# Sparse attention and experts on one core: local queries in a block-diagonal tile of their own, filled by GpSimd, and their transfers on ACT's queue

## Chip, cores and metric

One core of a Trainium2 chip. The metric is the device time of one execution in microseconds (us); lower is better. Times are medians of runs of the same program.

## What is computed

Eight batches, eight heads, 576 positions, head size 64. Heads 0 to 3 see a local window of 32 keys, heads 4 to 7 every 32nd key. The result of attention is read as 4608 tokens of 512 values, each of which goes to one of eight experts (512 to 1024, ReLU, back to 512), scaled by its gate. All is in fp32.

```python
scores = scale * np.matmul(q, k.transpose(0, 1, 3, 2))
mask_local = (rel >= 0) & (rel < stride)                      # stride 32, heads 0 to 3
mask_strided = (rel >= 0) & (pos[None, :] % stride == pos[:, None] % stride)
attn = softmax(np.where(masks, scores, -1e9)); x = attn @ v   # x as (4608, 512)
e = argmax(x @ w_gate); gate = softmax(x @ w_gate)[e]
out = gate * (np.maximum(x @ w1[e], 0.0) @ w2[e])
```

## The kernel before

**Tasks.** Attention is 40 tasks: batch b from 0 to 7, and in each five PSUM banks k from 0 to 4 (`BANK_PAIRS`, L54). Task n is 5 x b + k. Banks 0 and 1 hold the local scores of two heads each (heads 0 and 1, heads 2 and 3), banks 2 to 4 the last local blocks and the strided scores. Each task goes through three stages:

- `stage_s` (L388): TensorE adds the mask into the bank by a matmul (L391), then the scores. For local banks this is `wide` (L396): per block j of 32 queries one matmul, whose weights are 128 rows x 64 columns: the queries of head 0 in the upper 64 rows of 32 columns, of head 1 in the lower 64 rows of the other 32, zeros elsewhere (block diagonal). Each of these fp32 matmuls shows as two passes, so a task has 32. Then `softmax` (L337): VectorE's maximum and subtract, ACT's exponent, VectorE's sum and reciprocal, GpSimd's multiply of 128x512 (L350).
- `stage_t` (L438): four transposes of the probabilities (L441), copied out of PSUM by ACT (L443, L444, L447).
- `av_local` (L457, matmuls at L466) and `av_strided` (L470): probabilities times values, into xT.

**Where the local queries lie before.** For each of the two local banks there is one fixed tile `qkl[k]` (L355): 512 columns for head 0's queries, 512 for head 1's, then 544 of keys. The halves that must be zero are cleared once (L358 on VectorE, L359 on GpSimd). A load is three transfers on SP's queue (L369 to L371): the lower 64 rows of the second queries and keys in one, the upper 64 rows of the first queries, the upper 64 rows of the keys. The host has laid the queries out so that block j is every 16th column; `wide` reads its weights with that step:

```python
q = qkl[k][:, 0:2 * LQ].rearrange("p (q j) -> p q j", j=LB)      # LB = 16
nc.tensor.matmul(sb[64 * i:64 * i + 64, col:col + 64], q[:, :, j], qkl[k][:, k0:k0 + 64], ...)
```

**What sets the order.** TensorE's order is that of the loop at L803, written by hand: in turn i, `stage_t` of task i - 3, steps of routing, `stage_s` of task i, the values of task i - 4, a filling of expert work from the fifth batch on. The loads of queries and keys for task i + 5 are called right behind `stage_s` of task i (L821), those of values at L831. The other engines' queues, ACT, VectorE, GpSimd and SP, are put in order by a scheduler that goes by its own estimates of time; each engine then works its queue strictly in turn. `raw` tiles of expert weights (1 MB each, L204) are loaded by SP too, and split by `wsplit` (L209) into a rounded part (a cast on ACT, L212) and a rest (a subtract on VectorE, L213). Two raw and two split tiles exist in this part. Behind attention come the windows of the experts (`window`, L255) and eight slots for what is left over (`slot`, L872).

## Time and profile before

| | us |
|---|---|
| median of 3 runs | 691.83 |
| lowest, highest | 690.89, 695.33 |
| the profiled execution | 688.08 |
| its span in the trace | 686.2 |
| attention with its fillings, about | 0 to 215 |
| experts, about | 215 to 686 |

Times in the trace count from the start of its span; 1.9 us of the profiled execution lie outside it. PE is TensorE's matmuls, PEld its weight loads, DVE VectorE, ACT ScalarE, POOL GpSimd, SP SyncE; a q behind a name is that engine's queue of issues. A line number is that of the kernel above. In the trace a wait is put down to the event that ended it.

### The profile page before, as it was taken

How to read it: one execution, taken by the hardware profiler on the slowest of the kernel's cores; microseconds unless marked ns; L12 is line 12 of the kernel's file. 1: busy time of each engine (PE TensorE's matmuls, PEld its weight loads, DVE VectorE, ACT ScalarE, POOL GpSimd, SP SyncE). 2: the span in 40 equal slices, each digit the busy share in tenths (PEclk: the TensorE clock that was granted, in tenths of full speed). 3: DMA queues.
4: the chain of work that ended last, by engine and by line, in shares of the span. 5: the costliest groups of instructions: out<-in, count | busy, mean ns of one | idle time of the engine just before them, and what ended most of it. 6: DMA issues, size and time to landing. Idle time of an engine off the chain costs nothing.

```text
span 686.2 us, 14770 instructions
## 1 busy us (share of the span) xinstructions
PE 648.9 (95%) x5996; PEld 542.4 (79%) x5996; DVE 431.2 (63%) x796; ACT 354.5 (52%) x617; POOL 150.7 (22%) x168
## 2 busy tenths in 40 slices
PE   4999999799889899999999999999999999999997
PEld 3876768587778688897888988878888878988885
DVE  5667878567835579796336775346675248683364
ACT  1556666565555544564337574246473247572362
POOL 3222223511321302053005132022032041100021
PEclk9899999999999999999999999999999999999999
DMA  9879998985645657469327867337675257664140
GB/s 281 244 225 262 331 307 247 349 300 169 217 176 206 240 187 251 159 238 342 140 92 266 296 245 261 118 124 262 261 257 208 107 191 264 258 218 170 66 180 21
DMA packets 36695, 149.85 MB, mean 218 GB/s; under 512 B 5261, under 2 KB 5645, under 8 KB 26384
## 3 DMA queue, kind: packets, MB, share of 16 engines
q1 hardware_dynamic: 24576, 118.50, 51.1%
q0 software_dynamic: 6432, 20.26, 8.1%
q10 hardware_dynamic: 5616, 10.12, 4.1%
q8 instruction: 48, 0.79, 0.5%
q14 instruction: 23, 0.19, 0.1%
HBM read 129.69 MB, written 20.22 MB: 218 GB/s over the span
## 4 chain that ended last, share of the span: by engine, by line
PE 74%; issue 12%; DVE 5%; ACT 4%; DMA 2%; POOL 1%; POOLq 1%; SPq 0%; another core or an unknown queue 0%
PE t L287 8%; PE t L289 8%; PE t L288 8%; PE y L276 6%; PE y L278 6%; PE y L277 6%; PE s L399 4%; PE t L441 2%; PE s L412 2%; PE v L455 2%; PE v L466 2%; PE s L276 2%; PE s L278 2%; PE s L277 2%; PE v L265 2%
## 5 line engine op out<-in xcount | busy, mean ns | idle before, releaser
L213 DVE TENSOR_TENSOR wlo<-raw,whi 128x1024 fp32r<-128x1024 f32 x160 | 192.7, 1222 | 86.9 <-ACT whi L212 75.6
L212 ACT CAST whi<-raw 128x1024 fp32r<-128x1024 f32 x160 | 163.2, 1050 | 67.1 <-PE s L278 26.1
L287 PE MATMUL t<-xh,whi 128*128 128x256 f32 (+1 forms) x384 | 125.2, 327 | 1.9 <-ACT xh L221 1.3
L288 PE MATMUL t<-xl,whi 128*128 128x256 f32 (+1 forms) x384 | 123.8, 323 | 0.3 <-DVE xl L222 0.3
L289 PE MATMUL t<-xh,wlo 128*128 128x256 f32 (+1 forms) x384 | 123.4, 322 | 0.1
L292 ACT ACTIVATE hh<-t 128x256 fp32r<-128x256 f32 (+1 forms) x96 | 43.5, 453 | 115.1 <-PE t L289 109.2
L293 DVE SCALAR_TENSOR_TENSOR hl<-t,hh 128x256 fp32r<-128x256 f32 (+1 forms) x96 | 49.0, 510 | 75.6 <-ACT hh L292 75.2
L287 PEld LDWEIGHTS t<-xh,whi 128*128 128x128 f32 x384 | 72.4, 189 | 9.8 <-ACT xh L221 1.8
L288 PEld LDWEIGHTS t<-xl,whi 128*128 128x128 f32 x384 | 72.6, 189 | 7.2 <-DVE xl L222 0.7
L289 PEld LDWEIGHTS t<-xh,wlo 128*128 128x128 f32 x384 | 72.5, 189 | 6.4 <-DVE wlo L213 0.9
L276 PE MATMUL y<-whi,hh 128*128 128x512 f32 x192 | 76.2, 397 | 0.0
L277 PE MATMUL y<-wlo,hh 128*128 128x512 f32 x192 | 75.0, 391 | 0.0
L278 PE MATMUL y<-whi,hl 128*128 128x512 f32 x192 | 75.0, 396 | 0.0
L248 POOL DMA_INDIRECT out_dram<-y,oids x24 | 26.9, 1121 | 215.1 <-DVE y L247 166.5
L350 POOL TENSOR_TENSOR prob<-prob,ri 128x512 f32<-128x512 f32 x40 | 42.5, 1062 | 121.8 <-DVE ri L349 94.1
L155 ACT COPY xT<-v 128x270 f32<-128x270 f32 (+1 forms) x80 | 30.0, 481 | 29.0 <-PE v L455 13.0
L278 PEld LDWEIGHTS y<-whi,hl 128*128 128x128 f32 x192 | 35.6, 188 | 8.3
L276 PEld LDWEIGHTS y<-whi,hh 128*128 128x128 f32 x192 | 36.0, 188 | 6.7 <-ACT hh L292 0.7
L277 PEld LDWEIGHTS y<-wlo,hh 128*128 128x128 f32 x192 | 36.1, 188 | 5.7
L346 DVE TENSOR_REDUCE sm<-prob 128x8 f32<-128x512 f32 x40 | 27.3, 683 | 20.6 <-ACT prob L344 20.4
L340 DVE TENSOR_REDUCE nm<-s 128x8 f32<-128x512 f32 x40 | 27.3, 683 | 18.8 <-PE s L399 14.2
L344 ACT ACTIVATE prob<-prob 128x512 f32<-128x512 f32 x40 | 25.2, 631 | 22.9 <-DVE prob L343 22.1
(173 smaller groups left out, 1167.2 us busy)
## 6 DMA issues: line engine op xcount, KB each, us to landing
raw<-in_wcat_dram SPq DMA_DIRECT2D x80, 1024.0 KB, 6.5
xd<-xr ACTq DMA_DIRECT2D x36, 264.0 KB, 4.8
vl<-in_vv_dram SPq DMA_DIRECT2D x16, 512.0 KB, 6.5
qkl<-in_qk_dram SPq DMA_DIRECT2D x16, 264.0 KB, 3.8
vt<-in_vv_dram SPq DMA_DIRECT2D x16, 256.0 KB, 4.7
qk<-in_qk_dram SPq DMA_DIRECT2D x8, 484.0 KB, 5.5
qk<-in_qk_dram SPq DMA_DIRECT2D x8, 432.0 KB, 4.9
qk<-in_qk_dram SPq DMA_DIRECT2D x8, 396.0 KB, 6.3
```

What stands on the lines that cost most here:

```text
L155: nc.scalar.copy(out=out, in_=in_)
L212: nc.scalar.copy(out=hi[:, sl], in_=raw[:, sl])
L213: i = nc.vector.tensor_tensor(out=lo[:, sl], in0=raw[:, sl], in1=hi[:, sl].bitcast(F32), op=ALU.subtract)
L276: nc.tensor.matmul(yb[t], hh[:, ts], whi[:, w], start=(j == 0), stop=False)
L277: nc.tensor.matmul(yb[t], hh[:, ts], wlo[:, w], start=False, stop=False)
L278: nc.tensor.matmul(yb[t], hl[:, ts], whi[:, w], start=False, stop=(j == 7))
L287: nc.tensor.matmul(hb[:, 0:n], whi[:, w], xh[:, dc, :], start=(dc == 0), stop=False)
L288: nc.tensor.matmul(hb[:, 0:n], whi[:, w], xl[:, dc, :], start=False, stop=False)
L289: nc.tensor.matmul(hb[:, 0:n], wlo[:, w], xh[:, dc, :], start=False, stop=(dc == 3))
L292: nc.scalar.activation(out=hh[:, 0:n], in_=hb[:, 0:n], func=AF.Relu)
L293: nc.vector.scalar_tensor_tensor(out=hl[:, 0:n], in0=hb[:, 0:n], scalar=0.0, in1=hh[:, 0:n].bitcast(F32), op0=ALU.max, op1=ALU.subtract)
L350: lastp[0] = nc.gpsimd.tensor_tensor(out=pv, in0=pv, in1=ri.unsqueeze(2).broadcast_to([128, 8, 64]), op=ALU.mult)
```

## The change

- The local queries and keys come in one transfer of 128 rows x 1056 columns per task into `qkl[k]`, without gaps for zeros. For batch 0 SP issues it, from batch 1 on ACT.
- A new tile `qbd[k]` per local bank holds the block diagonal, block by block: 16 blocks of 64 columns. It is cleared once by VectorE. A new function `spread` copies each head's 64 rows of queries into their places by GpSimd, two copies of 64x512 per task; it is called for task i + 2 behind `stage_s` of task i, and for tasks 0 and 1 ahead of the loop.
- `wide` reads its weights from one block of `qbd[k]`, 64 columns in one run, and its keys from `qkl[k]`. The host no longer permutes the queries.
- The tiles of the other banks' queries and values become one per bank instead of three in rotation, and one small tile of the slot tables becomes a scratch tile.

```diff
--- before.py
+++ after.py
@@ -41,6 +41,7 @@
 CHW = 2 * 1024
 LAG_T = 3
 LAG_AV = 4
+AHEAD = 2
 EXP = (0, 2, 4, 6)
 EG = NG // 2
 EARLY = (3, 1, 2)
@@ -306,7 +307,7 @@
         return window(e, [ids[:, t, e:e + 1] for t in tr], [oids[:, t, e:e + 1] for t in tr], gpool, xpool, ypool)
 
     with ExitStack() as actx:
-        inp = actx.enter_context(tc.tile_pool(name="inp", bufs=NBK - 2))
+        inp = actx.enter_context(tc.tile_pool(name="inp", bufs=1))
         loc = actx.enter_context(tc.tile_pool(name="loc", bufs=1))
         inv = actx.enter_context(tc.tile_pool(name="inv", bufs=NV))
         probs = actx.enter_context(tc.tile_pool(name="probs", bufs=LAG_T + 2))
@@ -352,11 +353,11 @@
 
         loaded = {}
 
-        qkl = [loc.tile([128, 2 * LQ + LK], F32, name=f"qkl{k}") for k in range(2)]
+        qkl = [loc.tile([128, LQ + LK], F32, name=f"qkl{k}") for k in range(2)]
+        qbd = [loc.tile([128, LB, 2 * QB], F32, name=f"qbd{k}") for k in range(2)]
         pTl = [loc.tile([128, 2, 512], F32, name=f"pTl{k}") for k in range(2)]
         for k in range(2):
-            nc.vector.memset(qkl[k][64:128, 0:LQ], 0.0)
-            nc.gpsimd.memset(qkl[k][0:64, LQ:2 * LQ], 0.0)
+            nc.vector.memset(qbd[k].rearrange("p j q -> p (j q)"), 0.0)
         for k in range(2):
             nc.gpsimd.memset(pTl[k][64:128, 0, :], 0.0)
             nc.gpsimd.memset(pTl[k][0:64, 1, :], 0.0)
@@ -365,19 +366,24 @@
             if i < len(tasks):
                 b, k = tasks[i]
                 if k < 2:
-                    o = QKO[k]
-                    nc.sync.dma_start(out=qkl[k][64:128, LQ:], in_=qk[b, 64:128, o:o + LQ + LK])
-                    nc.sync.dma_start(out=qkl[k][0:64, 0:LQ], in_=qk[b, 0:64, o:o + LQ])
-                    nc.sync.dma_start(out=qkl[k][0:64, 2 * LQ:], in_=qk[b, 0:64, o + LQ:o + LQ + LK])
+                    (nc.scalar if b else nc.sync).dma_start(out=qkl[k], in_=qk[b, :, QKO[k]:QKO[k + 1]])
                     return
-                t = inp.tile([128, max(QKW[2:])], F32, name="qk")
+                t = inp.tile([128, QKW[k]], F32, name=f"qk{k}")
                 loaded[b, "qk", k] = t
                 nc.sync.dma_start(out=t[:, 0:QKW[k]], in_=qk[b, :, QKO[k]:QKO[k + 1]])
+
+        def spread(i):
+            if i < len(tasks) and tasks[i][1] < 2:
+                k = tasks[i][1]
+                for h in range(2):
+                    hs = slice(64 * h, 64 * h + 64)
+                    nc.gpsimd.tensor_copy(out=qbd[k][hs, :, QB * h:QB * h + QB],
+                                          in_=qkl[k][hs, 0:LQ].rearrange("p (j q) -> p j q", q=QB))
 
         def load_v(i):
             if i < len(tasks):
                 b, k = tasks[i]
-                t = inv.tile([128, VVW[0]], F32, name="vl", bufs=2) if k < 2 else inv.tile([128, max(VVW[2:])], F32, name="vt", bufs=3)
+                t = inv.tile([128, VVW[0]], F32, name="vl", bufs=2) if k < 2 else inv.tile([128, VVW[k]], F32, name=f"vt{k}", bufs=1)
                 loaded[b, "v", k] = t
                 nc.sync.dma_start(out=t[:, 0:VVW[k]], in_=vv[b, :, VVO[k]:VVO[k + 1]])
 
@@ -394,9 +400,8 @@
             at = QK[k][0]
 
             def wide(j, i, col, last):
-                q = qkl[k][:, 0:2 * LQ].rearrange("p (q j) -> p q j", j=LB)
-                k0 = 2 * LQ + QB * j
-                nc.tensor.matmul(sb[64 * i:64 * i + 64, col:col + 64], q[:, :, j], qkl[k][:, k0:k0 + 64],
+                k0 = LQ + QB * j
+                nc.tensor.matmul(sb[64 * i:64 * i + 64, col:col + 64], qbd[k][:, j, :], qkl[k][:, k0:k0 + 64],
                                  start=False, stop=last, tile_position=(0, 64 * i))
 
             def local(o0, nb, i, h, j, col, last):
@@ -654,7 +659,7 @@
         def slot_tables():
             rem = rt.tile([128, E], F32, name="rem")
             nc.vector.tensor_scalar(out=rem, in0=cnt, scalar1=-float(BASE), scalar2=0.0, op0=ALU.add, op1=ALU.max)
-            it128 = rt.tile([128, 32], F32, name="it128")
+            it128 = scratch(32)
             nc.vector.tensor_scalar(out=it128, in0=iota_sb[:, 0:32], scalar1=128.0, scalar2=None, op0=ALU.mult)
             cmp = scratch(E * 32).rearrange("p (e k) -> p e k", k=32)
             nc.vector.tensor_tensor(out=cmp, in0=rem.unsqueeze(2).broadcast_to([128, E, 32]),
@@ -787,9 +792,11 @@
 
         nc.scalar.dma_start(out=cst0, in_=blob0)
         load_qk(0)
+        spread(0)
         nc.vector.tensor_copy(out=identb, in_=ident)
         make_masks()
         load_qk(1)
+        spread(1)
         load_qk(2)
         load_v(0)
         load_qk(3)
@@ -818,6 +825,7 @@
                 if i < nt:
                     filling()
                     pvs[i] = stage_s(*tasks[i])
+                    spread(i + AHEAD)
                     load_qk(i + NBK)
                 if 0 <= ia < nt:
                     if k == 1:
@@ -1026,7 +1034,6 @@
             o += QKO[k]
             if key == "l":
                 parts = [lq[:, k, :, 0:LQ], lk[:, k, :, 0:LK]]
-                parts[0] = parts[0].reshape(B, 128, LB, QB).transpose(0, 1, 3, 2).reshape(B, 128, LQ)
             elif key[0] == "lx":
                 parts = [lq[:, key[1], :, LB * QB:], lk[:, key[1], :, LB * QB:]]
             elif key[0] == "s":
```

Where the scheduler puts the instructions now, at three places. GpSimd's queue at the start; qkl_133 and qkl_134 are the two local tiles (qbd_135 and qbd_136 the new ones), each pair of copies is one call of `spread`, ISA is the change of GpSimd's library, and the multiplies of L350 (now L351) go by task from 0. Before:

```order
L359 MEMSET qkl_133 64x512
L359 MEMSET qkl_134 64x512
L361 MEMSET pTl_135 64x512
L362 MEMSET pTl_135 64x512
L361 MEMSET pTl_136 64x512
L362 MEMSET pTl_136 64x512
L334 MEMSET xr 1x528
L335 DMA xd<-xr 16x1x33
L350 ISA
L350 TENSOR_TENSOR prob<-prob,ri 128x512 x9
```

Now, from the row of L335 (now L336) on:

```order
L336 DMA xd<-xr 16x1x33
L380 COPY qbd_135<-qkl_133 64x16x32 x2
L380 COPY qbd_136<-qkl_134 64x16x32 x2
L380 COPY qbd_135<-qkl_133 64x16x32 x2
L351 ISA
L351 TENSOR_TENSOR prob<-prob,ri 128x512 x3
L380 COPY qbd_136<-qkl_134 64x16x32 x2
L351 TENSOR_TENSOR prob<-prob,ri 128x512
L380 COPY qbd_135<-qkl_133 64x16x32 x2
L351 TENSOR_TENSOR prob<-prob,ri 128x512 x2
L380 COPY qbd_136<-qkl_134 64x16x32 x2
L351 TENSOR_TENSOR prob<-prob,ri 128x512 x3
```

The copies for tasks 0, 1 and 5 stand ahead of the library's change and of the multiply of task 0; those for task 6 ahead of the multiply of task 3, for task 10 ahead of that of task 4, for task 11 ahead of that of task 6. Further on, the copies for task 15 stand right ahead of the multiply of task 10, those for 21 of 16, for 31 of 26.

SP's queue from the loads of V in batch 0 on; vl and vt are values, qk the strided banks' queries and keys, raw is expert weights. Before, no load of raw stands in the first four batches:

```order
L382 DMA vt<-in_vv_dram 128x512
L369 DMA qkl_133<-in_qk_dram 64x1056
L370 DMA qkl_133<-in_qk_dram 64x512
L371 DMA qkl_133<-in_qk_dram 64x544
L369 DMA qkl_134<-in_qk_dram 64x1056
L370 DMA qkl_134<-in_qk_dram 64x512
L371 DMA qkl_134<-in_qk_dram 64x544
L375 DMA qk<-in_qk_dram 128x968
L375 DMA qk<-in_qk_dram 128x792
L375 DMA qk<-in_qk_dram 128x864
```

Now:

```order
L388 DMA vt_177<-in_vv_dram 128x512
L373 DMA qk_274<-in_qk_dram 128x968
L388 DMA vt_360<-in_vv_dram 128x512
L205 DMA raw<-in_wcat_dram 128x2048 x2
L373 DMA qk_314<-in_qk_dram 128x792
L373 DMA qk_358<-in_qk_dram 128x864
L205 DMA raw<-in_wcat_dram 128x2048
L388 DMA vl<-in_vv_dram 128x1024 x2
L373 DMA qk_516<-in_qk_dram 128x968
L205 DMA raw<-in_wcat_dram 128x2048
```

The local loads are gone from here, and four loads of expert weights now stand among the transfers for batches 1 and 2.

ACT's queue at the start; the exponents of L344 (now L345) go by task from 0, pTl is the copy of a local task's transposes, whi the cast of expert weights. Before:

```order
L344 ACT_TABLE_LOAD
L344 ACTIVATE prob<-prob 128x512 x2
L155 COPY pTl_135<-t 64x512
L344 ACTIVATE prob<-prob 128x512
L155 COPY pTl_135<-t 64x512
L155 COPY pTl_136<-t 64x512 x2
L344 ACTIVATE prob<-prob 128x512
```

Now:

```order
L369 DMA qkl_133<-in_qk_dram 128x1056
L345 ACT_TABLE_LOAD
L345 ACTIVATE prob<-prob 128x512 x2
L369 DMA qkl_134<-in_qk_dram 128x1056
L345 ACTIVATE prob<-prob 128x512
L156 COPY pTl_137<-t 64x512 x2
L213 CAST whi<-raw 128x1024 x2
L156 COPY pTl_138<-t 64x512 x2
L213 CAST whi<-raw 128x1024
L345 ACTIVATE prob<-prob 128x512
```

The transfers for tasks 5 and 6 stand ahead of the exponents of tasks 0 and 2, and three casts of expert weights ahead of that of task 3; a fourth follows the exponent of task 5.

## Rows read from the trace of the kernel before

**Rows 1.** The page: its first line, and its first section's line with the busy time, share of the span and instructions of each engine.
```profile
span 686.2 us, 14770 instructions
...
PE 648.9 (95%) x5996; PEld 542.4 (79%) x5996; DVE 431.2 (63%) x796; ACT 354.5 (52%) x617; POOL 150.7 (22%) x168
```

**Rows 2.** The table by stretch: start and end, length, then busy us and number of instructions of PE, PEld, DVE, ACT and POOL, TensorE's granted clock (1.00 is full), the DMA engines' busy share, GB/s. The stretches are batches 1 to 5 of attention, batches 6 and 7, and what follows.
```profile
22.00:42.00 20.00, 18.91 (x384) 14.45 (x383) 14.61 (x37) 11.22 (x25) 6.29 (x7) 1.00 0.80 243
42.00:62.00 20.00, 19.53 (x390) 14.25 (x388) 13.18 (x33) 11.47 (x26) 5.63 (x8) 1.00 0.84 254
62.00:84.00 22.00, 20.67 (x422) 16.87 (x421) 19.51 (x57) 14.58 (x31) 6.14 (x11) 1.00 0.89 289
84.00:104.00 20.00, 19.08 (x391) 14.56 (x391) 14.07 (x36) 12.96 (x29) 5.29 (x8) 1.00 0.94 299
104.00:125.00 21.00, 19.34 (x416) 16.25 (x415) 18.01 (x59) 14.42 (x31) 7.45 (x12) 1.00 0.91 297
125.00:168.00 43.00, 39.41 (x524) 32.51 (x522) 27.11 (x69) 22.63 (x46) 11.74 (x16) 1.00 0.79 260
168.00:215.00 47.00, 42.27 (x586) 36.25 (x587) 29.95 (x65) 26.19 (x49) 11.69 (x13) 0.96 0.53 184
215.00:686.00 471.00, 456.56 (x2719) 387.10 (x2713) 283.41 (x414) 234.98 (x377) 88.76 (x81) 1.00 0.57 203
```

**Rows 3.** TensorE's timeline: start, length in us, engine, line, operation, tiles, shapes, number of passes, and in brackets the idle time ahead with what ended it. In this order: scores of task 0, transposes of tasks 0, 3, 4 and 5, scores of task 10, the local values of batch 1 (L466), transposes of task 10, scores and transposes of task 16, the same of task 26.
```profile
6.92 2.11 PE L399 MATMUL s<-qkl 128*64 128x64 f32 x32 [1.67 <-DMA qkl<-in_qk_dram]
...
15.60 1.11 PE L441 MATMUL t<-cst,prob 128*128 128x128 f32 x4 [2.54 <-POOL prob L350]
...
26.47 0.66 PE L441 MATMUL t<-cst,prob 128*128 128x128 f32 x4
...
29.25 0.66 PE L441 MATMUL t<-cst,prob 128*128 128x128 f32 x4
...
31.95 0.66 PE L441 MATMUL t<-cst,prob 128*128 128x128 f32 x4
...
42.34 2.06 PE L399 MATMUL s<-qkl 128*64 128x64 f32 x32
44.24 2.04 PE L466 MATMUL v<-pTl,vl 128*64 128x64 f32 x64
...
52.12 0.66 PE L441 MATMUL t<-cst,prob 128*128 128x128 f32 x4
...
68.22 2.07 PE L399 MATMUL s<-qkl 128*64 128x64 f32 x32
...
77.56 0.66 PE L441 MATMUL t<-cst,prob 128*128 128x128 f32 x4 [0.45 <-POOL prob L350]
...
109.87 2.06 PE L399 MATMUL s<-qkl 128*64 128x64 f32 x32
...
118.68 0.66 PE L441 MATMUL t<-cst,prob 128*128 128x128 f32 x4
```

**Rows 4.** GpSimd's timeline at the start (columns as above): two memsets of 64x512, each half of the time given, and the first multiply of probabilities. Then, from the instructions of line 350, the change of GpSimd's library: number, shortest, median and longest in ns, first and last start in us.
```profile
0.76 0.98 POOL L359 MEMSET qkl<- 64x512 f32 x2 [0.29 <-POOLq L1072]
...
14.51 1.03 POOL L350 TENSOR_TENSOR prob<-prob,ri 128x512 f32<-128x512 f32 x1 [8.97 <-DVE ri L349]
...
L350 POOLq MODIFY_POOL_CONFIG  x2: 55/55/55, 5.5 to 5.6; - x2
```

**Rows 5.** Transfers. Four rows of the table by stretch (columns as in Rows 2). From the list of DMA issues: out, in, queue, number, KB of one, median us from issue to landing, for the whole run; then one row of that list for 10 to 12 us. From the instructions of line 369: number, ns of the issue (shortest, median, longest), and at the end the time from issue to landing of its pieces of 264 KB, in us.
```profile
10.00:12.00 2.00, 2.00 (x39) 1.67 (x39) 0.79 (x2) 0.63 (x1) 0.00 (x0) 1.00 1.02 408
12.00:14.00 2.00, 1.06 (x40) 0.84 (x39) 2.00 (x5) 0.39 (x1) 0.00 (x0) 1.00 1.04 422
16.00:18.00 2.00, 2.00 (x27) 1.38 (x27) 0.10 (x1) 1.22 (x3) 1.04 (x1) 0.50 1.01 214
18.00:20.00 2.00, 2.00 (x23) 1.38 (x19) 1.83 (x4) 0.68 (x2) 0.00 (x0) 0.50 1.05 235
...
xd<-xr ACTq DMA_DIRECT2D x36, 264.0 KB, 4.8
...
qkl<-in_qk_dram SPq DMA_DIRECT2D x16, 136.0 KB, 7.3
...
qkl<-in_qk_dram SPq DMA_DIRECT2D x1, 128.0 KB, 9.3
...
L369 SPq DMA_DIRECT2D qkl<-in_qk_dram x16: 465/472/596, 0.8 to 138.1; - x16
...
DMA to landing us min/median/max: 3.4/3.8/4.0
```

**Rows 6.** The instructions that read the tile of raw expert weights, all through the run: number, ns (shortest, median, longest), first and last start in us.
```profile
L212 ACT CAST whi<-raw x160: 1035/1048/1081, 90.7 to 670.9; 128x1024 fp32r<-128x1024 f32 x160
L213 DVE TENSOR_TENSOR wlo<-raw,whi x160: 1173/1220/1301, 92.9 to 672.9; 128x1024 fp32r<-128x1024 f32 x160
```

**Rows 7.** The stretch from 120 to 140: its row of the table, a wait on TensorE's timeline, and from SP's timeline the first two loads of expert weights.
```profile
120.00:140.00 20.00, 15.14 (x213) 11.45 (x209) 10.88 (x34) 10.04 (x23) 8.63 (x11) 1.00 1.00 343
...
135.28 0.55 PE L265 MATMUL v<-cst,xg 128*128 128x128 f32 x3 [1.36 <-DMA xg<-xd,eids]
...
82.73 0.33 SPq L204 DMA_DIRECT2D raw<-in_wcat_dram  x1
...
123.15 0.42 SPq L204 DMA_DIRECT2D raw<-in_wcat_dram  x1
```

## Prediction

> **What bounds the kernel now.** Read the page first [rows 1]: TensorE is busy 95% of the span, no other engine above 63%. Busy time of pipelined matmuls is no proof, so next comes the table by stretch [rows 2], one row per batch of attention: TensorE is busy 94% to 98% in the three rows from 22 to 84, 95% and 92% up to 125, and still 92% and 90% from 125 to 215, where expert matmuls are mixed in. After 215 it is busy 97%, in an order fixed by hand. So the work is one TensorE stream: a matmul that gets shorter should pull the end forward, wherever the stream doesn't then wait for somebody else. The same table says who that would be: VectorE is busy 19.51 of 22.00 in 62:84 and 18.01 of 21.00 in 104:125, against 13.18 of 20.00 in 42:62.
>
> Then one step of the stream on TensorE's timeline [rows 3]. I call S(n) the scores of task n, T(n) its transposes, M(n) the multiply that GpSimd does between them, F(n) the two new fills; n is 5 x batch + bank, and local tasks have n = 0, 1, 5, 6, 10, 11 and so on. S(10), 32 passes of 64 columns, takes 2.06 us. The 64 passes of L466 right behind it, with weights of the same 128x64 shape and 64 moving columns too, take 2.04, which is 1.02 for 32. What differs is how the weights lie: L399 reads each weight row with a step of 16 elements, L466 in one run. The change makes L399's weights one run.
>
> **The change part by part.** The sum is made against the profiled execution: 688.08 us, of which the span is 686.2. That is 3.75 us under the median of the three runs shown (691.83), and I carry the difference in us over to the median.
>
> *Matmuls.* 16 local tasks x (2.06 - 1.02) = 16.6 us less TensorE time, which is the ceiling. It does not all reach the end. Batches 0 and 1 (four stages) go under in the start, below. In batches 2 and 4 VectorE has room, so 2.1 each. In batches 3 and 5 VectorE's share (89%, 86%) leaves about half: 1.2 each (between 0 and 2.1). Batches 6 and 7: TensorE's idle there is 10%, so 3.7 of 4.2. Together 10.3.
>
> *The fills on GpSimd, steady part.* 32 copies of 64x512 from one SBUF place to another. No row shows one. Bounds: the memset of that shape, 0.52 each, and the multiply of 128x512 with two inputs, 1.04 [rows 4]. I take 0.55, since the memset has the same shape; a pair is 1.1 (1.0 to 2.1). GpSimd is busy 22%, so the time itself is covered. What is not covered is the order: GpSimd works its queue strictly in turn, and as the pieces of the order show, a fill stands ahead of the multiply of an earlier task. F(15) stands ahead of M(10), and it waits for a transfer that can only be issued when S(10) has ended. Counted from the end of S(10): issue 0.47 [rows 5], landing L, fills 1.1, multiply 1.04, two handovers of 0.1. L is 540 KB on ACT's queue, not shown. Bounds: 3.4 (the fastest 264 KB piece) and 9.3 (a 128 KB piece issued in 10:12 [rows 5]). I take 4.8, the median of the 264 KB stores that ACT issues [rows 5], as it is the only row on that queue. That is 7.6 us. What is allowed: T(10) begins 52.12 - 42.34 = 9.8 after S(10) begins, less 2.1 for two shorter stages, less 1.0 for S(10) itself: 6.7. So T(10) is 0.9 late. For S(26) to T(26) it is 118.68 - 109.87 = 8.8, less 1.04, less 1.0: 6.8, late by 0.8; but batch 5 is counted at half anyway, so half of that. For S(16) to T(16), 77.56 - 68.22, the same way: 7.3, late by 0.3. Loss: about 1.5, so 10.3 becomes 8.8. Every microsecond of L above 4.8 costs about four here, one per batch from 2 to 5.
>
> *The start.* Here the change moves the most, and mostly unasked. On GpSimd F(0), F(1) and F(5) come ahead of M(0). My estimates: the first local block, now one transfer issued at 0.76, lands near 4.5 and S(0) ends near 7.1 instead of 9.03. That opens the transfer for F(5): 0.47 + 4.8 puts it at 12.4, the fills end at 13.5. Between them and M(0) stands the reload of GpSimd's library (the row ISA in the pieces, MODIFY_POOL_CONFIG in the trace). Before, it stood at 5.5, and the 8.97 us until the multiply at 14.51, which waited for VectorE, hid it [rows 4]. Now it stands behind F(5) and nothing hides it. Its cost is between 0 and the 8.9 that hid it; no row is like it, so I take the middle, 4.5. M(0) then starts at 18.0 and T(0) at 19.2 instead of 15.60 [rows 3].
>
> The Trainium skill (GPSIMD Engine Reference, section 2.1, Instruction dispatch) says that the first call after such a load waits about 6 us for code, with nothing in the profile to see. The trace agrees as far as it can, since 8.9 us cover it; with 6 the start would be 1.5 later and the forecast 687.5.
>
> The second thing at the start: four blocks of expert weights, first issued at 82.73 and 123.15 before [rows 7], are now issued in the first batches, and their split is set between the softmax steps of tasks 3 to 6: four casts of 1.05 on ACT, four subtracts of 1.22 on VectorE [rows 6]. The first block comes about 7.3 MB into the stream. At the 408 to 422 GB/s that whole 128-partition rows reach in 10:14 [rows 5] it lands near 20.7, just before ACT asks for it; at the 214 to 235 of 16:20, where the half-height local pieces ran [rows 5], it would be later than 25, and the softmax of task 3 would wait for it. With 20.7 two subtracts delay task 3 and two casts stand before its exponent: T(3) near 30.5 instead of 26.47. Then M(4) stands behind F(10): S(5) ends near 27, plus 0.47 + 4.8 + 1.1 + 1.04 is 34.5, T(4) follows at 34.7 instead of 29.25, and T(5) is about 5 late. From there the stream is full, so the 5 us stay: loss 5 (2.5 with L 3.4 and no reload, 9.5 with the reload at 8.9), with the shorter stages of batches 0 and 1 already in it.
>
> *Given back later.* In 120:140 TensorE is busy only 15.14 of 20 while the DMA engines are busy 1.00 [rows 7]; 1.36 of its idle is a gather that lands late. A weight block is issued right there at 123.15, and others follow. These are gone, and the local transfers take less DMA time. I credit 2 of the 4.9 idle (0 to 4.9).
>
> *Nothing for the rest.* 14 transfers x 0.47 are 6.6 us of ACT's sequencer, and ACT is busy 52%; they stand behind the exponent of a task whose scores must have ended anyway. If not, exponents wait. SP loses 48 issues; what is behind them, V and the strided blocks, is early already. Buffers per bank instead of in rotation: three banks shared three buffers in turn, so each gets the one that it had. The clears on VectorE are twice as wide and stand ahead of casts that wait for the first constants; if they outlast that wait, the masks start as much later. The small scratch tile costs an instruction's place.
>
> Sum: -8.8 + 5 - 2 = -5.8: 682.3 against 688.08, and 686.0 against the median.
>
> **The rivals.** *Nearly all of it arrives.* The transfer lands in 3.4, the reload is short, the start loses 1, no fill is late, VectorE keeps up, and the idle of 120:140 goes: -(4 x 2.1 + 4.2) + 1 - 4.9 = -16.5, so 675.3. For it: TensorE is the fullest engine in every row [rows 2]. Against: VectorE at 89% in 62:84.
>
> *The start takes it all.* Reload 8.9 and the first weight block at 25, nothing given back: start 9.5, steady 8.8: +0.7, so 692.5. For it: DMA engines are full all through 10:20 [rows 5]. Against: half-height pieces, the slow ones, are what goes.
>
> *Slower: the fills hold the multiplies.* GpSimd's place in the order decides: L is 7.3, the median of the 136 KB pieces [rows 5], not 4.8, and a fill with its multiply is 10.1 behind the scores. T(10) is then 3.4 late, T(16) 2.8, T(26) 3.3, and batch 4, whose pairs I did not work out, is put at 1.6: 11 us in four batches. The start loses 2.5 twice more, 5 + 5; nothing is given back: -12.6 + 11 + 10 = +8.4, so 700.2. It decides from L near 6 on, where the forecast's gain is used up. The Trainium skill (DMA: Bandwidth & Descriptors, section Issuing engines are not separate DMA queues) speaks for it: transfers from ACT and SP run on the same 16 engines and interleave, so another queue saves only issue time. The trace agrees that ACT's queue is no faster lane: 264 KB take 4.8 there and at most 4.0 from SP [rows 5].
>
> That the matmuls do not get shorter, because the step is not what doubles them, would leave only the losses; it counts with this rival. Against it: the shapes of L399 and L466 are alike but for the step.
>
> **How the numbers follow.** About what a measurement of this kernel can tell from no change is 1%, 6.9 us. Forecast (-11 to -1): 0.45. Nearly all: 0.25. Start takes it: 0.15. Slower: 0.15. Faster by over 1%: all of the second and 0.4 of the first, 0.43. Slower by over 1%: most of the last, 0.13. Within 1%: the rest, 0.44. The range goes from the second case to most of the slower one: 676 to 697; the forecast's own is 681 to 691.
>
> **What would show it.** Right: L399 takes about 1.02 for 32 passes; the first multiply starts between 16 and 20 with a gap behind F(5) that waits for nothing; the first weight cast near 21; TensorE waits for GpSimd's multiply once in batches 2 and 5; fewer idle us in 120:140. Wrong: M(0) on time at 14.5; S(10) still 2 us; waits on the fill's transfer in every batch, with L above 6; VectorE at over 95% from 62 to 125.

## The result: slower by 0.9%, outside the range

| | before | after |
|---|---|---|
| median of 20 runs each, us | 693.24 | 701.25 |
| profiled execution, us | 688.08 | 703.36 |
| ratio, with its 95% interval | | 1.0094 (1.0072 to 1.0115) |

The forecast was 686.0, the range 676 to 697. Ratios leave disturbed runs out, so here and below they need not be the quotient of the medians. The two profiled executions lie 15.4 us of span apart, the medians 8.0: before's profile is from the low end of its runs, after's from above its median. Of the traces I therefore read where a delay arises, and take the size of the whole from timed runs.

The page of after, the same two lines as in [rows 1]:

```profile
span 701.6 us, 14739 instructions
...
PE 641.3 (91%) x5978; PEld 535.5 (76%) x5996; DVE 436.4 (62%) x796; ACT 354.2 (50%) x617; POOL 170.3 (24%) x198
```

TensorE is busy 7.6 us less than in [rows 1] (18 of its records are missing, a few us at most), and the span is 15.4 longer: it waits 23 us more. The table by stretch, columns and stretches as in [rows 2] up to the end of attention; 120:140 answers [rows 7]:

```profile
22.00:42.00 20.00, 13.14 (x296) 10.68 (x293) 13.89 (x25) 10.36 (x16) 6.72 (x9) 0.88 0.69 250
42.00:62.00 20.00, 17.85 (x420) 13.40 (x421) 14.04 (x35) 13.17 (x32) 7.92 (x11) 1.00 0.92 323
62.00:84.00 22.00, 20.00 (x427) 15.19 (x423) 19.25 (x57) 12.56 (x30) 9.27 (x17) 1.00 0.79 250
84.00:104.00 20.00, 17.99 (x442) 14.01 (x441) 14.54 (x37) 13.84 (x33) 6.74 (x11) 1.00 0.87 312
104.00:125.00 21.00, 18.16 (x334) 13.46 (x338) 17.17 (x53) 10.29 (x22) 9.30 (x17) 0.92 0.70 222
125.00:168.00 43.00, 35.80 (x584) 28.96 (x588) 25.24 (x67) 24.14 (x54) 16.13 (x23) 0.96 0.68 225
168.00:215.00 47.00, 40.65 (x536) 35.78 (x540) 30.42 (x68) 25.94 (x48) 11.64 (x12) 0.89 0.52 177
...
120.00:140.00 20.00, 15.44 (x360) 11.83 (x359) 15.38 (x43) 12.41 (x28) 9.60 (x12) 1.00 0.89 298
```

The hole is in the first row: 13.14 us busy of 20, against 18.91. It opens on GpSimd. Its timeline at the start, answering [rows 4]:

```profile
17.05 1.28 POOL L380 COPY qbd<-qkl 64x512 f32<-64x512 f32 x2 [8.89 <-DMA qkl<-in_qk_dram]
18.43 3.04 POOL L351 TENSOR_TENSOR prob<-prob,ri 128x512 f32<-128x512 f32 x3
21.41 1.27 POOL L380 COPY qbd<-qkl 64x512 f32<-64x512 f32 x2
29.61 1.04 POOL L351 TENSOR_TENSOR prob<-prob,ri 128x512 f32<-128x512 f32 x1 [6.93 <-DVE ri L350]
34.47 1.92 POOL L380 COPY qbd<-qkl 64x512 f32<-64x512 f32 x2 [3.82 <-DMA qkl<-in_qk_dram]
36.47 2.04 POOL L351 TENSOR_TENSOR prob<-prob,ri 128x512 f32<-128x512 f32 x2
```

The first row is F(5), which waits 8.89 us for its transfer with M(0) behind it; the fifth is F(10), with M(4) behind it. TensorE's transposes of tasks 0, 3 and 4, and the scores of task 5, answering [rows 3]:

```profile
19.52 1.12 PE L446 MATMUL t<-cst,prob 128*128 128x128 f32 x4 [7.25 <-POOL prob L351]
...
25.83 1.15 PE L404 MATMUL s<-qkl,qbd 128*64 128x64 f32 x32
30.70 0.66 PE L446 MATMUL t<-cst,prob 128*128 128x128 f32 x4 [1.85 <-POOL prob L351]
...
37.56 1.12 PE L446 MATMUL t<-cst,prob 128*128 128x128 f32 x4 [4.91 <-POOL prob L351]
```

T(0) waits 7.25 us for the multiply, T(4) 4.91; M(0) is 3.9 later than before, M(4) 10.6, M(8) 8.8. The last transposes cost 1.12 instead of 0.66: the granted clock is 0.50, the 1.2 GHz level, in 18:22 and 38:40, each time after TensorE had waited. The first of the two is nothing new: before, the clock is 0.50 in 16:20 [rows 5] and T(0) takes 1.11. From M(8) on, the delay to the trace of before lies between +4.9 and +10.9 us and has no trend: +6.9 at the first scatter, GpSimd's write of finished rows into the result (183.7 before), and +8.6 at M(39). It is +12.1 at the gather of rows that stood at 299.9.

### The profile page after: what moved, and what is told of

It reads as the page before. It is cut to its first block, busy times and chain, and to the rows that moved or that the text cites. A ratio compares the mean times of both kernels' runs of the same rounds, so it can differ in the third digit from the quotient of the medians.

```text
span 701.6 us, 14739 instructions
## 1 busy us (share of the span) xinstructions
PE 641.3 (91%) x5978; PEld 535.5 (76%) x5996; DVE 436.4 (62%) x796; ACT 354.2 (50%) x617; POOL 170.3 (24%) x198
## 4 chain that ended last, share of the span: by engine, by line
PE 61%; issue 12%; DVE 2%; ACT 1%; POOL 1%; DMA 1%; POOLq 1%; another core or an unknown queue 0%; ACTq 0%
PE t L288 8%; PE t L290 7%; PE t L289 7%; PE y L279 6%; PE y L277 6%; PE y L278 6%; PE s L277 2%; PE s L279 2%; PE v L266 2%; PE s L278 2%; PE s L919 1%; PE s L921 1%; PE s L920 1%; PE t L902 1%; PE v L912 1%
## 5 line engine op out<-in xcount | busy, mean ns | idle before, releaser
L351 POOL TENSOR_TENSOR prob<-prob,ri 128x512 f32<-128x512 f32 x40 | 41.6, 1043 | 76.1 <-DVE ri L350 57.5
L446 PE MATMUL t<-cst,prob 128*128 128x128 f32 x160 | 27.2, 297 | 15.2 <-POOL prob L351 15.2
L345 ACT ACTIVATE prob<-prob 128x512 f32<-128x512 f32 x40 | 25.3, 632 | 28.8 <-DVE prob L344 25.4
L230 POOL DMA_INDIRECT xg<-xd,ids x24 | 31.0, 1291 | 32.9 <-ACT xh L222 20.0
L156 ACT COPY xT<-v 128x270 f32<-128x270 f32 (+1 forms) x80 | 29.5, 476 | 17.3 <-PE v L460 12.6
```

The lines of the kernel that those rows point to most:

```text
L230: lastp[0] = nc.gpsimd.indirect_dma_start(out=xg, out_offset=None, in_=xd[0:rows, :], in_offset=bass.IndirectOffsetOnAxis(ap=idc, axis=0))
L351: lastp[0] = nc.gpsimd.tensor_tensor(out=pv, in0=pv, in1=ri.unsqueeze(2).broadcast_to([128, 8, 64]), op=ALU.mult)
```

## The experiments

Chips differ: the kernel before took 681 to 693 us on those used. Each ratio is therefore against the kernel before on the same chip. Even so the changed kernel itself gave 1.0094 on one chip and 1.0183 on another, so ratios are compared within one chip unless it is said.

**Do short matmuls help by themselves?** Three versions of the kernel before, without the new tile and copies. `step16` is the control: the weights keep their step of 16 elements, the keys come in one transfer. `step4` lays the queries with a step of 4 elements (16 bytes). `zeros` has the host lay the block diagonal with its zeros in memory, one transfer of 803 KB on SP.

```diff
-                q = qkl[k][:, 0:2 * LQ].rearrange("p (q j) -> p q j", j=LB)
+                q = qkl[k][:, 0:2 * LQ].rearrange("p (g q s) -> p g q s", q=2 * QB, s=ST)   # step16, step4
+                q = qkl[k][:, 0:2 * LQ].rearrange("p (j q) -> p j q", j=LB)                 # zeros
```

> The kernel before, with one edit that is a control for the next two: the keys of both heads come in one transfer of 128 rows, the queries in two of 64 rows as they were; the weights are still read with a step of 16 elements. No copies on GpSimd, nothing on ACT's queue. All theories: as before, ratio 0.995 to 1.005; the score matmuls stay at 2.06 us for 32 passes.

> As the control, but the host lays the queries out so that the weights of a block are read with a step of 4 elements (16 bytes) instead of 16 (64 bytes); the transfers of queries then write runs of 512 bytes. Still no copies on GpSimd. Theory A (TensorE's stream is the bound, and what the changed kernel lost it lost through the fills and the order that came with them): if a step of 16 bytes is already cheap, 32 passes take about 1.1 us and 16 x 0.95 = 15 us of matmul go; 8 to 15 of it reach the end, ratio 0.978 to 0.988. If a step of 16 bytes costs as much as 64, nothing moves. Theory B (the chain of softmax on VectorE, ACT and GpSimd paces the batches, and TensorE's granted clock falls when it has gaps): the matmuls get shorter, the kernel gains less than 3 us, ratio 0.996 to 1.004.

> The kernel before, but the block diagonal comes from memory with its zeros: one transfer of 128 rows x 1568 columns (803 KB) per local task on SP, weights of a block in one run, no clears, no copies on GpSimd. 16 x 264 KB = 4.2 MB more are moved, some 10 us of full DMA bandwidth at the 410 GB/s that whole rows reach. Theory A: 32 passes take 1.0 to 1.15 us as in the changed kernel; 8 to 15 us gained where the DMA has room, 2 to 5 lost in the start, where it has none: ratio 0.98 to 0.995. Theory B: within 3 us of the kernel before, or slower by the transfers at the start, ratio 1.00 to 1.01.

Measured: 1.0035 (1.0008 to 1.0061), 1.0053 (1.0022 to 1.0083) and 0.9981 (0.9960 to 1.0003). The instructions of the local scores, weight loads and passes: number, shortest, median and longest ns. `step16`, `step4`, `zeros`:

```profile
L405 PEld LDWEIGHTS s<-qkl x512: 184/207/229, 7.3 to 184.6; 128*64 128x64 f32 x171
L405 PE MATMUL s<-qkl x512: 270/277/385, 7.4 to 184.6; 128*64 128x64 f32 x171
```
```profile
L405 PEld LDWEIGHTS s<-qkl x512: 192/217/218, 7.9 to 188.0; 128*64 128x64 f32 x171
```
```profile
L396 PEld LDWEIGHTS s<-qkl x512: 132/138/231, 7.4 to 178.6; 128*64 128x64 f32 x171
L396 PE MATMUL s<-qkl x512: 222/222/369, 7.4 to 178.7; 128*64 128x64 f32 x171
```

The step is what doubles the stage, and 16 bytes are as slow as 64. But the saved time hardly reaches the end. 16 x (2.06 - 1.15) = 14.6 us of TensorE's stream go; its busy time falls by 7.0 from `step16` to `zeros` (645.2 to 638.2 on the pages), the span by 2.5 (680.6 to 678.1), the medians by 3.2. `zeros` also moves 4.2 MB more, and no run has short matmuls without either those bytes or the copies; part of what is missing may be their price. The rest is in these rows, columns as before, `step16` and then `zeros`:

```profile
0.00:22.00 22.00, 11.96 (x185) 9.22 (x186) 11.91 (x33) 6.00 (x9) 7.61 (x15) 0.92 0.92 292
22.00:125.00 103.00, 96.51 (x1988) 75.52 (x1985) 80.66 (x218) 65.56 (x139) 30.92 (x44) 0.98 0.86 290
...
168.00:215.00 47.00, 43.55 (x581) 37.03 (x581) 33.29 (x78) 27.23 (x53) 12.50 (x13) 1.00 0.54 195
```
```profile
0.00:22.00 22.00, 12.01 (x171) 9.01 (x173) 10.16 (x30) 5.62 (x9) 6.52 (x13) 0.85 0.89 338
22.00:125.00 103.00, 92.73 (x2058) 71.09 (x2057) 83.70 (x226) 67.66 (x142) 31.56 (x44) 0.97 0.90 328
...
168.00:215.00 47.00, 42.77 (x613) 36.14 (x612) 32.33 (x67) 27.57 (x51) 13.30 (x16) 0.93 0.54 189
```

In 22:125 TensorE waits 10.3 us instead of 6.5; in the other two stretches it runs more of its work at the lower clock (0.85 instead of 0.92, 0.93 instead of 1.00), so that busy time does not fall with the work.

**Is the work on the path at all?** `zeros` with 32 useless passes ahead of each local task's scores.

```diff
+                for j in range(LB):
+                    nc.tensor.matmul(sb[...], q[:, j], qkl[k][:, k0:k0 + 64], start=True, stop=True, ...)
```

> The kernel with zeros from memory, plus useless work: ahead of the mask each local task does its 32 passes of scores once more into the same bank, where the mask then overwrites them. That is 16 x 1.0 to 1.15 = 16 to 18 us more of TensorE, about what the change took away. Theory A (TensorE's stream is the bound in attention): 10 us or more slower than without, ratio to before 1.012 to 1.025. Theory B (in the batches TensorE waits for the softmax chain anyway, and where it waits its granted clock falls): most of it is hidden or given back by a clock that stays up: 0 to 5 us slower, ratio 0.998 to 1.006, and a mean granted clock above the 0.980 of the kernel with zeros.

1.0159 (1.0105 to 1.0213). Against `zeros` that is 1.0159 - 0.9981 = 1.8%, some 12 us for 16 to 18 added. The two ran on different chips, so this is rough; their traces agree with it, M(39) is 11.7 us later in `padded`. Work that is added counts by about two thirds; of work that is taken away `zeros` got back a fifth (3.2 of 14.6, against `step16` on its own chip).

**GpSimd's order or the early weights?** Three edits of the changed kernel: the copies for task n stand behind the multiply of task n - 4 (`fill_behind`); loads of expert weights are held behind the loads of V called before them (`weights_held`); and both.

```diff
+                    if i - FB in muls:                  # FB = 4
+                        issue_after(c, muls[i - FB])    # c: the copy
...
+        if lastl:
+            issue_after(d, lastl[-1])                   # d: the load of weights
```

> The changed kernel with one thing changed in the order: the copies for task n stand on GpSimd behind the multiply of task n-4 (they stood up to seven multiplies earlier). Everything else, the weights hoisted to the start among it, stays. Theory A: the first multiply starts at 15.2, when its reciprocal is done, not at 18.4; those of tasks 3 and 4 no longer stand behind a transfer; of the 8.8 us that the changed kernel is late after batch 1 at least 5 go, and the waits at tasks 10, 12, 21 and 24 go: ratio to the kernel before 0.985 to 1.000, 6 to 14 us better than the changed kernel. Theory C (it is the four hoisted blocks of expert weights, with their transfers and their casts and subtracts, that delay the start; the fills only show it): the multiplies of tasks 3 and 4 stay 5 us late, and less than 4 us are gained on the changed kernel.

> The changed kernel, but a block of expert weights may be issued on SP only behind the loads of values that the program calls ahead of it: the four blocks that had moved into batches 1 and 2 come late in attention. The copies on GpSimd stay where the change puts them. Theory A (the copies hold the multiplies): the multiply of task 0 still starts near 18.4, because it stands behind a transfer, but tasks 3 and 4 lose the casts and subtracts (4 x 1.05 on ACT, 4 x 1.22 on VectorE) and the transfers for tasks 10 and 11 land sooner; 2 to 4 us better than the changed kernel, 698 to 699 against 701 in its scale, ratio to before 1.003 to 1.007. Theory C (the hoisted weights are the delay): 5 to 8 us better, ratio 0.997 to 1.002.

> The changed kernel with both: the copies for task n behind the multiply of task n-4, and the expert weights held back. What is left of the change is the local transfers on ACT's queue, 32 copies on GpSimd and the short matmuls. If the fills' order and the hoisted weights are all that the change lost, the kernel comes out where the one with zeros from memory did, ratio 0.993 to 1.000. If the copies or ACT's queue cost something by themselves, it stays at 1.004 or above.

1.0101 (1.0053 to 1.0150), 1.0731 (1.0693 to 1.0768) and 1.0586 (1.0542 to 1.0631). `fill_behind` missed its forecast; the changed kernel did not run on that chip, so what the edit is worth there isn't known. Holding the weights overshot: the filled-in expert matmuls starved for them (18.4 us of TensorE's waits before 230 in `weights_held`), so the totals of the last two say nothing on the start. They were made anew, with each load behind the load of V that it followed in the order before (`WHEN`): with the copies behind (`placed`), without (`weights_placed`), and `placed` with the local transfers on SP (`on_sp`); `sp_only` makes that last edit alone.

```diff
-                    (nc.scalar if b else nc.sync).dma_start(out=qkl[k], in_=qk[b, :, QKO[k]:QKO[k + 1]])
+                    nc.sync.dma_start(out=qkl[k], in_=qk[b, :, QKO[k]:QKO[k + 1]])    # on_sp, sp_only
...
+        if wn[0] <= len(WHEN):                          # WHEN = (20, 30, 32, 33, 35, 35, 37, 37)
+            issue_after(d, lastl[min(WHEN[wn[0] - 1], len(lastl)) - 1])
```

> The changed kernel with the copies for task n behind the multiply of task n-4, and each of the first eight blocks of expert weights issued no earlier than in the kernel before (behind the same number of loads of values: 20, 30, 32, 33, 35, 35, 37, 37). In the run that held them back until their own place in the program, attention was 6 to 10 us ahead of the kernel before up to task 30, with a clock of 1.00 from 22 to 125, and then starved for weights. If the loss of the changed kernel is the fills' order and the early weights, and nothing else, those 6 to 10 us stay: ratio 0.985 to 0.993. If the weights that come in at 80 and 120 collide with the rest as they did before, 2 to 5 us stay: 0.993 to 0.998. At 1.000 or above something else is at work.

> The changed kernel with the expert weights no earlier than before, as in the last, but the copies on GpSimd where the change has them. With the fills ahead of the multiplies attention was 3 to 5 us behind the kernel before, and 4 us ahead of the changed one, in the run that held the weights back. Expected: 4 to 5 us better than the changed kernel, ratio 1.002 to 1.006; the distance to the last kernel, 6 to 12 us, is what the order of the copies costs.

> As the first of these (copies behind the multiply of task n-4, weights no earlier than before), but all transfers of local queries and keys on SP's queue instead of ACT's. If ACT's queue has a worth of its own (SP free for others, or the reverse: exponents that wait behind issues), it shows here: more than 3 us to either side. If what it did was only to move the weights and the fills forward, the two are the same within 0.4%.

> The changed kernel with one edit: the transfers of local queries and keys from batch 1 on stay on SP's queue. Nothing is pinned, but without the empty places on SP the scheduler puts the first expert weights behind the loads of batch 3 and the copies for tasks 5 and 6 behind the multiply of task 2, by itself. If the queue is the part of the change that brought the loss at the start (through the order), most of the 8.8 us after batch 1 go: ratio 0.990 to 1.000. If the copies on GpSimd cost it whatever the queue: 1.004 or above.

1.0117 (1.0075 to 1.0158), 1.0231 (1.0196 to 1.0265), 0.9971 (0.9940 to 1.0003) and 1.0049 (1.0020 to 1.0078). Late weights alone win nothing in the total. In the trace they do win at the start: M(8) is 4.7 us later than in the kernel before, against 8.6 in the changed kernel's own trace on that chip. F(10) and M(4) of `weights_placed`:

```profile
30.44 1.27 POOL L386 COPY qbd<-qkl 64x512 f32<-64x512 f32 x2 [3.02 <-DMA qkl<-in_qk_dram]
31.80 2.04 POOL L357 TENSOR_TENSOR prob<-prob,ri 128x512 f32<-128x512 f32 x2
```

The gain is lost later, where the weights now come: at M(19) the delay is 3.3 us, at M(20) 8.5, at M(39) 11.9.

The edits of `placed` and `on_sp` differ by the queue alone, and `placed` is 9.0 us slower (689.67 against 680.72), more than the 3 us that were to show that the queue has a worth of its own. At M(19) the two are still level, both 2.6 us ahead of the kernel before. They part where the first late weights arrive. ACT's first cast of them in `placed`, then in `on_sp`:

```profile
86.36 1.05 ACT L220 CAST whi<-raw 128x1024 fp32r<-128x1024 f32 x1 [3.24 <-DMA raw<-in_wcat_dram]
```
```profile
84.01 1.05 ACT L220 CAST whi<-raw 128x1024 fp32r<-128x1024 f32 x1 [1.80 <-POOL xr L520]
```

In `placed` ACT stands 3.24 us before a cast whose transfer has not landed, with the exponent of task 20 behind it, and M(20) starts at 91.3; in `on_sp` the wait is not for the weights, and M(20) starts at 87.6. It is the same pattern on another engine: an instruction that waits for a transfer, ahead of work that is due. Which part of the 9.0 us this one place makes was not tested.

`sp_only` comes close to the kernel before with one line. In it the scheduler, unasked, also moves the copies for tasks 5 and 6 behind M(2) and the first expert weights to 36 us (the changed kernel issues them at 16 on that chip), so it doesn't tell the queue from the order. Its 1.0049 lies in the range that was put for copies that cost the time whatever the queue, with an interval that reaches out of it. The three runs below tell the two apart, for the start.

**The deciding three**, on one chip: the changed kernel again, `sp_only`, `fill_behind`.

> The changed kernel itself, as a control beside the next two on the same chip. Ratio to the kernel before between 1.007 and 1.020: 1.0094 was measured, but the profiled execution was 15.3 us longer than that of before (1.022).

> The changed kernel with all local transfers on SP's queue, once more (1.0049 elsewhere). If the queue, through the order that it sets off, is the larger part of the loss, it is 3 us or more faster than the control on this chip; if the copies on GpSimd cost the time whatever the queue, it is within 2 us of it.

> The changed kernel with the copies for task n behind the multiply of task n-4, once more (1.0101 elsewhere). If the place of the copies in GpSimd's order is the larger part, it is 3 to 6 us faster than the control; by the ratios so far it would be no faster at all.

Medians 693.49, 684.06, 683.32 against 681.0: 1.0183 (1.0154 to 1.0211), 1.0039 (1.0010 to 1.0068), 1.0039 (1.0014 to 1.0064). Each edit alone takes 9.4 or 10.2 of the 12.5 us lost on this chip. GpSimd's timelines at the start, in that order:

```profile
15.66 1.28 POOL L380 COPY qbd<-qkl 64x512 f32<-64x512 f32 x2 [7.40 <-DMA qkl<-in_qk_dram]
17.03 3.04 POOL L351 TENSOR_TENSOR prob<-prob,ri 128x512 f32<-128x512 f32 x3
...
33.66 2.23 POOL L380 COPY qbd<-qkl 64x512 f32<-64x512 f32 x2 [3.50 <-DMA qkl<-in_qk_dram]
35.97 2.04 POOL L351 TENSOR_TENSOR prob<-prob,ri 128x512 f32<-128x512 f32 x2
```
```profile
14.94 2.04 POOL L351 TENSOR_TENSOR prob<-prob,ri 128x512 f32<-128x512 f32 x2 [6.84 <-DVE ri L349]
...
18.37 2.59 POOL L380 COPY qbd<-qkl 64x512 f32<-64x512 f32 x4
24.04 1.04 POOL L351 TENSOR_TENSOR prob<-prob,ri 128x512 f32<-128x512 f32 x1 [3.07 <-DVE ri L350]
```
```profile
14.98 2.04 POOL L352 TENSOR_TENSOR prob<-prob,ri 128x512 f32<-128x512 f32 x2 [6.90 <-DVE ri L350]
...
18.41 2.59 POOL L382 COPY qbd<-qkl 64x512 f32<-64x512 f32 x4
24.02 1.04 POOL L352 TENSOR_TENSOR prob<-prob,ri 128x512 f32<-128x512 f32 x1 [3.02 <-DVE ri L351]
```

In the last two the multiplies stand ahead of the copies and wait for nothing but VectorE; no copy waits at 18.4. T(4) on TensorE, same order:

```profile
37.07 1.11 PE L446 MATMUL t<-cst,prob 128*128 128x128 f32 x4 [4.91 <-POOL prob L351]
```
```profile
27.02 0.66 PE L446 MATMUL t<-cst,prob 128*128 128x128 f32 x4
```
```profile
28.10 0.65 PE L450 MATMUL t<-cst,prob 128*128 128x128 f32 x4 [1.02 <-POOL prob L352]
```

T(4) is 10.0 and 9.0 us earlier, and the first scatter still 8.9 and 9.2. `fill_behind` keeps ACT's queue and the early weights (the first at 16.9), so on this chip neither is by itself the larger part of the loss; the place of the copies is. The queue set off that place, and with late weights it cost 9.0 us in another way, as `placed` shows. By the pages 528 KB land in a median of 5.6 us from ACT in `fill_behind` and 5.6 from SP in `sp_only`.

**The half clock and the gather.** `warm` puts useless matmuls into TensorE's waits ahead of T(0), T(3), T(4), T(10); `warm_gather` is `on_sp` with 24 of them ahead of the matmuls on the first gathered rows; `gather_later` is `on_sp`, and `before_later` the kernel before, with those matmuls two turns later.

```diff
+            for _ in range(WARM.get(NBK * b + k, 0)):   # warm: {0: 16, 3: 4, 4: 12, 10: 3}
+                nc.tensor.matmul(tb, identb, mask_b[:, 0].rearrange("p n k -> p (n k)"), start=True, stop=True)
...
-            for _ in range(4):                          # gather_later, before_later
+            for _ in range(6):
                 yield
```

> The changed kernel, with useless bf16 matmuls of 512 columns ahead of the transposes of tasks 0, 3, 4 and 10 (16, 4, 12 and 3 of them, 0.38 us each at full clock), into the bank that the transposes overwrite. They fill the waits of 7.25, 1.85, 4.91 and 1.23 us that TensorE has there. In the changed kernel the granted clock fell to half after the first and the third of these, for 16 to 24 and for 36 to 41 us. If the half clock follows the idle time and costs what the doubled durations show, the clock stays up there and the multiply of task 8 comes 2 to 5 us earlier, the kernel 2 to 5 us faster than the changed one. If the clock falls for another reason, or the stream waits for others behind these places, nothing is gained, and it may be 1 to 2 us slower.

> The same kernel as the first of these, but with four turns as before, and 24 useless bf16 matmuls of 512 columns (about 0.235 us each as measured, 5.6 us) in TensorE's stream ahead of the first matmuls on the gathered rows, where TensorE waited for 5.93 us and then ran at half clock to 137. If the half clock comes from the idleness, the granted clock stays at 1.00 through 140 and the stream is 2 to 2.5 us earlier behind this place; ratio 0.993 to 0.996 against 0.997 without. If the clock falls nonetheless, nothing is gained.

> The kernel with copies behind the multiply of task n-4, weights no earlier than before and all local transfers on SP (it was 0.3% faster than the kernel before), with one number changed: six turns of the loop instead of four between the gather of the first expert's rows and the first matmuls on them. If the gather takes the gain away, TensorE's wait of 5.9 us near 132 shrinks below 2 us, the clock near 132 to 137 stays at 1.00, and 4 to 7 us are gained: ratio to the kernel before 0.987 to 0.992. If the stream is paced elsewhere, the wait only moves: 0.995 to 1.000.

> The kernel before with the same one number: six turns instead of four. Its wait for the gather was 1.36 us in the first trace (4.5 in the control with merged keys). If the gather takes away only what the shorter matmuls bring, little is gained here: ratio 0.996 to 1.001. If it gains as much as the other, the two turns are a gain by themselves, and have nothing to do with the change.

`warm`: 1.0154 (1.0116 to 1.0193). The clock is 1.00 through 0:22, yet M(8) is only 1.5 us earlier than in after, and M(0), whose transfer landed sooner, was already 1.7 earlier: the half clock of the start follows the waits and costs little beside them. Its ratio can't be set against that of after, which didn't run on that chip. Moving the gathered matmuls later was a miss both times, 1.0066 (1.0039 to 1.0093) and 1.0075 (1.0045 to 1.0105). `warm_gather`: 0.9991 (0.9966 to 1.0015), no gain in the total. How a good start's lead is used up there for a time shows in `on_sp`, TensorE's first matmul on gathered rows and the stretch around it, and then the same in `warm_gather`:

```profile
131.94 0.45 PE L273 MATMUL v<-cst,xg 128*128 128x128 f32 x1 [5.93 <-DMA xg<-xd,eids]
...
125.00:140.00 15.00, 8.53 (x70) 6.88 (x69) 5.93 (x13) 5.50 (x11) 5.98 (x9) 0.66 0.75 279
```
```profile
130.91 0.27 PE L276 MATMUL v<-cst,xg 128*128 128x128 f32 x1
...
125.00:140.00 15.00, 13.64 (x190) 9.18 (x188) 6.99 (x14) 5.49 (x13) 7.55 (x11) 1.00 0.74 273
```

TensorE comes early and stands 5.93 us before a gather that lands when it lands (1.36 in [rows 7]); then it runs at a clock of 0.66 on the mean, in `warm_gather` at 1.00. The lead of `on_sp` goes from 5.4 us at M(28) to 1.2 at M(29). It is back at 6.1 by M(39), and 2.5 are left at the gather that stood at 299.9: what is lost for good goes behind attention (the last step below).

No version is clearly faster than before: `on_sp` and `zeros` are the best, both with 1 in the interval.

## Why the prediction was wrong, step by step

- **Matmuls**: right in kind, and mis-sized. 32 passes take 1.15 us, not 1.02, so the ceiling is 14.6 instead of 16.6.
- **What of it arrives (-8.8)**: wrong, and the largest miss. From task 8 to task 39 the delay went from +8.8 to +8.6; in `zeros`, without copies, 3.2 of 14.6 reached the end. "The work is one TensorE stream" took a busy share for proof that shorter work ends sooner. `padded` shows that the stream is near the pace from one side only: made shorter, it waits more and runs at the lower clock more. From `step16` to `zeros`, in 22:125, TensorE's waits for the multiplies go from 1.3 to 2.1 us, for ACT's copies from 2.9 to 3.7, for VectorE from 0.7 to 1.6; no run took one of them alone. Three waits for copies also came, M(10), M(12) and M(21) 2 to 3 us late each, of the kind that was foreseen with 0.9.
- **The start (+5)**: the mechanism was named, and the size is what failed: +8.8 by M(8). T(3) came at 30.70, where 30.5 was put. M(0) at 18.43 matched 18.0 by luck: three terms were off and cancel. S(0) ended at 9.09 instead of 7.1: its transfer landed at 5.1, the mask was added at 6.60 (its constants came at 5.28, before at 3.58), and these 32 passes took 1.98. For the landing I put 4.8, for the reload 4.5. The transfers took longer, as ACT's timeline shows:

```profile
9.19 0.33 ACTq L369 DMA_DIRECT2D qkl<-in_qk_dram  x1
...
22.55 1.99 ACT L213 CAST whi<-raw 128x1024 fp32r<-128x1024 f32 x2 [0.70 <-DMA raw<-in_wcat_dram]
...
27.07 0.33 ACTq L369 DMA_DIRECT2D qkl<-in_qk_dram  x1
```

  From 9.19 to the copies at 17.05 are 7.9 us, from 27.07 to 34.47 7.4, where 5.3 was put with the issue; the median landing over the run is 5.4. The second of them and the two copies (1.92 us instead of 1.1) put T(4) at 37.56 where 34.7 was forecast. And the reload showed no cost: the copies end at 18.33, M(0) starts at 18.43. The Trainium skill (GPSIMD Engine Reference, section 2.1, Instruction dispatch) has a first call after a load wait about 6 us; here the change of library stands between the copies and M(0), which are 0.1 apart, so the trace does not agree. Whether something was loaded during the wait for F(5) can't be seen.
- **The landing time L** was the mis-sized term of the start. The third rival named it ("decides from L near 6 on"), took 7.3 and came to 700.2, with a chance of 0.15. [Rows 5] held the better rows, 7.3 for the 136 KB pieces and 9.3 for the piece issued in that very stretch; I took 4.8 from ACT's stores, the row of the same queue instead of that of the same stretch. That rival's sum is not what happened either: it had 12.6 arrive and the copies take 11 of it, where the traces show a late start and no steady loss. Nor is it the stretch alone: with ACT's queue the transfer for F(10) takes 5.2 to 8.1 us in the five traces with early weights, and 4.2 to 4.9 in the four without.
- **The early weights**: right that they move and that they delay the start; the first cast came at 22.55, near the 21 that was named. Without them M(8) is 3.9 us less late (`weights_placed`, 4.7 against 8.6). With the copies behind the multiplies they cost only 1.0 there (`fill_behind` +1.4, `placed` +0.4). Placed late with ACT's queue they cost as much elsewhere: the totals of these two are no better for it.
- **Given back in 120:140 (-2)**: not seen. TensorE is busy 15.44 of 20, against 15.14 [rows 7], though with all some 8 us later the stretch holds other work; the first gather is issued 7.9 us later than before, a delay like those of M(25) and M(30), 8.3 and 7.4.
- **"After 215 in an order fixed by hand"**: wrong, and not a term of the sum. The scheduler orders the seam between attention and experts. In after, two transposes of gathered rows stand ahead of the `y` matmuls and wait; before, they stand behind (first after, then before):

```profile
278.40 0.30 PE L266 MATMUL v<-cst,xg 128*128 128x128 f32 x1 [1.14 <-DMA xg<-xd,ids]
279.19 0.33 PE L266 MATMUL v<-cst,xg 128*128 128x128 f32 x1 [0.49 <-DMA xg<-xd,ids]
...
280.34 0.78 PE L277 MATMUL y<-whi,hh 128*128 128x512 f32 x1
```
```profile
269.69 0.62 PE L278 MATMUL y<-whi,hl 128*128 128x512 f32 x2
270.15 0.60 PE L265 MATMUL v<-cst,xg 128*128 128x128 f32 x4
```

  The delay grows by 3.5 us between 232 and 300 in after. Against the same trace `sp_only` and `fill_behind` lose 2.7 and 1.4 there, and `zeros`, whose TensorE order is that of before, loses nothing. The order there is that of before in all versions of the kernel before with four turns, which lose nothing, and that of after in all versions of the changed kernel with four turns, which lose 1.2 to 3.6 us. So neither the queue nor the place of the copies or the weights tips it. What is left are parts that all of those share, such as the copies themselves and the changed tiles; no run took the seam alone. It is what I put the remaining 0.4% of those two down to, not shown.

So the sum failed at two terms. The -8.8 of shorter matmuls was not paid out: in the trace nothing of it shows between M(8) and M(39). The +5 of the start was 8.8, where copies that wait for transfers of 7.4 to 7.9 us stand ahead of multiplies, with early weights beside them. That this order is the larger part of the loss is shown on one chip, by `fill_behind` alone (10.2 of 12.5 us) and by `sp_only` with it (9.4). On the chip of the result, where the loss is 8.0, it was not repeated.

## To carry to other kernels

Where an engine works its queue in turn, an instruction that waits for a transfer belongs behind the work that is already due, and moving an issue to another queue can reorder a third engine: read its new order, and price each copy by the slowest landing of that very stretch. A busy share of 95% does not say what shorter work brings: here added work cost about two thirds of itself and removed work gave back a fifth. Ask what would be late next.

## What the chip did that was not expected

- A weight load of 128x64 fp32 takes 138 ns from one run of columns, 207 with a step of 64 bytes and 217 with one of 16; the Trainium skill (SBUF — State Buffer, section Door 1: The DMA port swizzle) says that an access pays when it goes on to a new line of 16 bytes, and puts the free step at up to 4 fp32 values. That crossing costs agrees; a step of 4 values is not free here, but as slow as one of 16.
- How long a transfer of 528 KB takes depends on the stretch more than on the queue. In the first 35 us it took 7.4 to 7.9 us from issue to use in after, and from issue to landing 5.9 to 7.0 from ACT in that kernel's second trace, 6.0 to 7.4 from SP in `sp_only` on the same chip; 4.2 from ACT in `placed` at 25 us, without early weights. The medians are 5.4 in after and 5.6 in `fill_behind` (ACT) and `sp_only` (SP).
